# A fused attention, mixer and gated-MLP kernel: the first stage's order written out, later transposes, weight splits on VectorE

## The chip, the cores and the metric

The kernel runs on one core of a Trainium2 chip. The metric is the device time of one execution in microseconds. Engines are called by their names: TensorE (PE), VectorE (DVE), ScalarE (ACT), GpSimd (POOL), and SyncE (SP), which here issues all DMAs.

## The reference

Eight batches of 576 tokens go through three blocks. Block-local attention in chunks of 64 tokens gives x; a mixer multiplies over tokens and over channels; a gated MLP with a spatial product gives the output.

```python
scores = scale * np.matmul(q_c, k_c.transpose(0, 1, 2, 4, 3))   # 8 heads, 9 chunks of 64
attn = np.exp(scores - np.max(scores, axis=-1, keepdims=True))
attn = attn / (np.sum(attn, axis=-1, keepdims=True) + 1e-09)
x = np.matmul(attn, v_c)                                        # to [B, 576, 512]
h = np.maximum(x.transpose(0, 2, 1) @ w_tok1, 0.0) @ w_tok2     # tokens 576 -> 256 -> 576
u = x + h.transpose(0, 2, 1)
x = u + np.maximum(u @ w_ch1, 0.0) @ w_ch2                      # channels 512 -> 1536 -> 512
h = np.maximum(x @ w_in, 0.0)                                   # 512 -> 1024, halves u and v
v_s = np.einsum('ts,bsd->btd', w_spatial, normalized(v)) + b_spatial[None, :, None]
out = (u * v_s) @ w_out
```

## The kernel before

**Pairs of halves.** A product of 32-bit accuracy is made of three f16 products: every operand is kept as a high half and a low half (value minus high half), and high·high, high·low and low·high are summed in PSUM. The weights come in double precision: each is read as two 32-bit words, put together to an f32 by bit operations and then split. `add_w` cuts them into chunks `W[0]` to `W[23]`: 0 and 1 are `t1w` (first token product), 2 and 3 `t2w`, 4 to 9 `c1w` (first channel product), 10 to 15 `c2w`, 16 to 19 `inw` (gate), 20 and 21 `otw` (output), 22 and 23 `spw` (spatial). A chunk has four steps, one per `w_tick` with two chunks in flight: `upper` (two VectorE operations, L127 and L129), `lower` (one, L133), `high` (ScalarE, L139) and `low`. In chunks 0 to 5 `low` is made by TensorE, as f32 identity times s (L149) minus f16 identity times the high half (L150), and evicted by ScalarE (L151); from chunk 6 on by one VectorE operation (L144). Chunks 0 to 19 are loaded into tiles that are still unused (vn, otw, spw, xb, xT) and are split during batch 0's channel products; 20 to 23 are loaded into parts of hb and are split later.

**Attention.** A batch has five groups g of 128 tokens (the last of 64). The groups of batches 0 and 1 go through `wide_steps`: score (TensorE, L380), shift (VectorE, a maximum and a subtraction, L387 and L388), expo (ScalarE), norm (VectorE, L397 to L400), turn (TensorE transposes, L405), turned (ScalarE), attend (TensorE, L416 and L418), out_hi (ScalarE, L425 and L426) and out_lo (VectorE, L431). Later batches go through `at_steps`, with L246 as the score and L302 as the attend product. Batch 0's five groups come first in the program, each three ticks behind the one ahead. All further groups are a list `order` of (5g + s, g, s) that `a_step` works off one step at a time.

**Batches.** Per batch: tok1 (L500, L504), tok2 (L477 with t2w), ch1 (12 outputs of 24 products, L477 with c1w), ch2 (L560), gate_v (L477 with inw), then tok1 of the next batch, then `gated` (spatial and gate_u, L477), tok2 of the next batch and proj (L657). ch1's output is evicted by ScalarE (high half, L550) and VectorE (low half, L551). PSUM is a pool `pm` of four two-bank tiles, handed out in turn to all of this.

**What sets the order.** Inside `tc.manual_schedule` the named engines issue in the order in which the code is written: TensorE from tok1 on, and SyncE for the first loads. Into TensorE's written order `pump` inserts attention steps and weight ticks: each product moves a planner's clock on by its columns / 2.4 + 2.5 ns, and an entry of `pumps` runs its step when the clock has come to its due time. The other engines, and TensorE ahead of tok1, are ordered by a scheduler from the program's order as priority and its own estimate of when inputs are ready. Each engine then issues strictly in the order so fixed.

Of the kernel before, what the change touches and what calls it, by code (L numbers as in the profile page):

```python
# [26 lines left out]
def mixer_kernel(ctx: ExitStack, tc, qk0, qk, v, wt1, wt2, wc1, wc2, win, wsp, bsp, wout, out):  # L27
# [58 lines left out]
    neg = gall[:, 4864:4992]  # L86
    W = []

# [7 lines left out]
    early = lambda i: FIRST[i] if i < 6 else CYCLE[i % 3] if i < 20 else ("h0", "h1")[i % 2]  # L96
# [18 lines left out]
    def w_steps(i):  # L115
# [39 lines left out]
    KW, LATE, BY_PE = 2, 20, 6  # L155
# [192 lines left out]
    one_v = v32.rearrange("p a b c d -> p (a b c d)")[:, 0:512].rearrange("p (c h d) -> p c h d", c=2, h=4)  # L348
# [13 lines left out]
    def wide_steps(g):  # L362
# [3 lines left out]
        if b == 0:  # L366
            raw, vals = first_qk[:, i * 1024:i * 1024 + 8 * n], first_v[:, 2 * i:2 * i + nc_]
        else:
            raw, vals = one_qk[:, 0:8 * n], one_v[:, 0:nc_]
# [73 lines left out]
    order = sorted((KA * g + s, g, s) for g in range(NT, NG) for s in range(NA))  # L443
    todo = [0]

    def a_step():
# [4 lines left out]
        for f in live[g][s]:  # L451
            f()
# [40 lines left out]
    def tok1():  # L493
# [8 lines left out]
        for m in range(2):  # L502
            for e in range(2):
                PE.matmul(out=pss[m], lhsT=t1w[:, e, col(4, m)], rhs=x16[:, 8], start=False, stop=(e == 1))  # L504
                pump(DM)
            last = ACT.activation(out=h1[:, m, 0], in_=pss[m], func=AF.Relu).ins  # L506
            DVE.scalar_tensor_tensor(out=h1[:, m, 1], in0=pss[m], scalar=0.0, in1=h1[:, m, 0],  # L507
                                     op0=ALU.max, op1=ALU.subtract)
# [16 lines left out]
    def tok2(m, x):  # L525
# [8 lines left out]
        first_residual(ps, m, x)  # L534
# [9 lines left out]
    def ch1(m):  # L544
# [5 lines left out]
        ACT.activation(out=hh, in_=ps, func=AF.Relu)  # L550
# [130 lines left out]
    with tc.manual_schedule(engines={mybir.EngineType.SP}):  # L681
# [3 lines left out]
        for i in range(2, 5):  # L685
            wide_qk(i)
# [3 lines left out]
    for tick in range(3 * 4 + 9):  # L690
# [4 lines left out]
        if tick >= 9:  # L695
            w_tick()
# [120 lines left out]
```

## Time and profile before

| | |
|---|---|
| median of 3 runs | 1179.11 us (1178.23 to 1180.81) |
| the profiled execution | 1178.89 us |
| its span, first to last instruction | 1177.1 us |
| TensorE busy | 1132.4 us (96%) |
| VectorE busy | 719.0 us (61%) |
| ScalarE busy | 424.9 us (36%) |
| GpSimd busy | 197.7 us (17%) |

Rows of the timeline give the start, the duration, the engine, the line of the code, the operation, the tiles (out<-in), shapes and count; in brackets stands how long the engine was idle before it and whose end released it. In the names, `gb` is the scratch tile of the weight splits and holds the identity, `hb` the hidden activations (and at first batch 0's q, k and v), `mp` any PSUM tile, `sd` scores and probabilities, `p` and `pT` the transposed probabilities, `xb` the residual stream's halves. Windows give each engine's busy time (and instructions) in a stretch, then TensorE's granted clock as a share of full speed, the share of the DMA engines and GB/s.

### The profile page before, as it was taken

Reading aid. Unit: us, or ns where it says so; the run is one execution under the profiler, and the core shown is the slowest. Engines: PE = TensorE matmul, PEld = TensorE weight load, DVE = VectorE, ACT = ScalarE, POOL = GpSimd, SP = SyncE. Lnnn points to the kernel's source line nnn. Section 1 sums busy time; section 2 is a strip of 40 time slices with the busy share of each in tenths; the row PEclk is TensorE's granted clock in tenths of the full one; section 3 lists DMA queues with packets and bytes.
Section 4 is the critical chain, followed back from the end, with each engine's and each line's share of the span. In section 5 each row is a group of like instructions: output and inputs, shape, how many; then the busy total and the mean of one; then the engine's idle time right before and its main releaser. Section 6 shows DMA issues by size and latency. Waiting matters only on the chain. (4 is left out here: it accounts for less than half of the span.)

```text
span 1177.1 us, 22164 instructions
## 1 busy us (share of the span) xinstructions
PE 1132.4 (96%) x9564; PEld 819.1 (70%) x9564; DVE 719.0 (61%) x1279; ACT 424.9 (36%) x658; POOL 197.7 (17%) x186
## 2 busy tenths in 40 slices
PE   5879998999999999999999999999999999999998
PEld 4457755788577875778667885778757786677765
DVE  6899889755676655875576555765656432442141
ACT  3544434443335424443344333354233422221121
POOL 0000013201220122211131013201222011200020
PEclk9999999999999999999999999999999999999999
DMA  9456252312223230232223122233201311000001
GB/s 326 167 190 223 60 185 46 72 46 55 63 46 90 68 68 27 63 91 50 68 46 81 46 61 57 46 81 64 73 28 46 55 28 36 1 1 1 10 28 45
DMA packets 87602, 83.55 MB, mean 71 GB/s; under 512 B 66128, under 2 KB 68432, under 8 KB 85200
## 3 DMA queue, kind: packets, MB, share of 16 engines
q1 hardware_dynamic: 87504, 82.14, 26.1%
q8 instruction: 75, 1.23, 0.4%
q14 instruction: 23, 0.19, 0.1%
HBM read 58.52 MB, written 9.44 MB: 58 GB/s over the span
## 5 line engine op out<-in xcount | busy, mean ns | idle before, releaser
L477 PE MATMUL mp<-xb,c1w 128*128 128x288 f16 x2304 | 288.9, 287 | 0.0
L560 PE MATMUL mp<-hb,c2w 128*128 128x288 f16 x2304 | 287.7, 286 | 0.0
L477 PEld LDWEIGHTS <-c1w 128*128 128x128 f16 x2304 | 224.8, 98 | 58.1
L560 PEld LDWEIGHTS <-c2w 128*128 128x128 f16 x2304 | 223.5, 98 | 55.8
L551 DVE SCALAR_TENSOR_TENSOR hb<-mp,hb 128x576 f16<-128x576 f32 x96 | 72.3, 753 | 103.5 <-ACT hb L550 103.3
L477 PE MATMUL mp<-spw,vn 128*128 128x288 f16 x896 | 117.9, 288 | 2.7 <-DVE xT L317 2.7
L477 PEld LDWEIGHTS <-vn 128*128 128x128 f16 x896 | 87.1, 99 | 26.3 <-PE mp L477 4.1
L550 ACT ACTIVATE hb<-mp 128x576 f16<-128x576 f32 x96 | 62.2, 648 | 108.8 <-PE mp L477 108.5
L477 PE MATMUL mp<-xb,inw 128*128 128x288 f16 x768 | 99.3, 286 | 0.0
L657 PE MATMUL mp<-otw,gb 128*128 128x512 f16 x432 | 96.0, 379 | 0.0
L477 PEld LDWEIGHTS <-inw 128*128 128x128 f16 x768 | 75.2, 98 | 20.4
L477 PE MATMUL mp<-inw,xb 128*128 128x512 f16 x384 | 86.0, 383 | 2.6 <-ACT xb L522 2.5
L281 POOL TENSOR_TENSOR p<-sd,p 128x512 f16<-128x512 f32 (+1 forms) x30 | 34.6, 1155 | 282.3 <-ACT p L278 271.1
L333 POOL TENSOR_TENSOR xh<-xT,xh 128x512 f16<-128x512 f32 x24 | 32.1, 1336 | 289.7 <-ACT xh L330 255.4
L657 PEld LDWEIGHTS <-gb 128*128 128x128 f16 x432 | 42.1, 98 | 47.9
L477 PEld LDWEIGHTS <-xb 128*128 128x128 f16 x384 | 37.6, 98 | 49.5 <-ACT xb L522 2.9
L521 DVE SCALAR_TENSOR_TENSOR rt<-mp,xT 128x576 f32<-128x576 f32 x32 | 24.2, 757 | 74.6 <-PE mp L560 74.1
L292 DVE SCALAR_TENSOR_TENSOR v<-v,v 128x512 f16<-128x512 f32 (+1 forms) x60 | 36.5, 634 | 40.7 <-ACT v L288 40.3
L596 DVE BATCH_NORM_STATS2 st<-vt 128x6 f32<-128x512 f32 (+1 forms) x40 | 27.6, 690 | 45.9 <-ACT vt L590 45.6
L523 POOL TENSOR_TENSOR xb<-rt,xb 128x576 f16<-128x576 f32 x21 | 29.4, 1400 | 153.2 <-ACT xb L522 153.2
L643 ACT ACTIVATE gb<-gt 128x576 f16<-128x576 f32 x32 | 21.8, 682 | 88.0 <-DVE gt L641 87.7
L477 PE MATMUL mp<-t2w,hb 128*128 128x288 f16 x384 | 51.2, 286 | 1.1 <-ACT hb L506 0.4
(147 smaller groups left out, 1367.5 us busy)
## 6 DMA issues: line engine op xcount, KB each, us to landing
qk<-in_qk SPq DMA_DIRECT2D x28, 512.0 KB, 3.9
v<-in_v SPq DMA_DIRECT2D x48, 256.0 KB, 3.9
out<-o SPq DMA_DIRECT2D x31, 256.0 KB, 2.0
vn<-in_wc SPq DMA_DIRECT2D x4, 1024.0 KB, 5.2
otw<-in_wc SPq DMA_DIRECT2D x3, 1024.0 KB, 6.5
spw<-in_wc SPq DMA_DIRECT2D x3, 1024.0 KB, 4.9
v<-in_v SPq DMA_DIRECT2D x20, 128.0 KB, 2.7
hb<-in_qk SPq DMA_DIRECT2D x4, 512.0 KB, 8.0
```

Source lines behind the costliest of these rows:

```text
L281: POOL.tensor_tensor(out=p16[rows, :, 1], in0=m["sd"][rows], in1=p16[rows, :, 0], op=ALU.subtract)
L292: DVE.scalar_tensor_tensor(out=hi_lo[:, :, 1 + e], in0=v_in[:, :, e], scalar=SX, in1=hi_lo[:, :, 3 * e], op0=ALU.mult, op1=ALU.subtract)
L333: POOL.tensor_tensor(out=m["lo"], in0=xT[:, :, tk], in1=m["hi"], op=ALU.subtract)
L477: PE.matmul(out=o, lhsT=l, rhs=r, start=(i == 0), stop=(i == len(seq) - 1))
L521: DVE.scalar_tensor_tensor(out=t, in0=ps, scalar=DN10, in1=two(x[:, m]), op0=ALU.mult, op1=ALU.add)
L523: eng.tensor_tensor(out=xl, in0=t, in1=xh, op=ALU.subtract)
L550: ACT.activation(out=hh, in_=ps, func=AF.Relu)
L551: DVE.scalar_tensor_tensor(out=hlo, in0=ps, scalar=0.0, in1=hh, op0=ALU.max, op1=ALU.subtract)
L560: PE.matmul(out=o, lhsT=c2w[:, a, k, mc], rhs=hb[:, k, r, s], start=(k + e == 0), stop=(k == 11 and e == 2))
L596: DVE.bn_stats(out=st[0:n], in_=t[0:n])
L643: ACT.activation(out=gh, in_=t, func=AF.Copy)
L657: PE.matmul(out=ps, lhsT=gb[:, l, k, tk], rhs=otw[:, r, k], start=(k == 0 and e == 0), stop=(k == 3 and e == 2))
```

## The change

Ahead of the first token product the order of all of TensorE, ScalarE, VectorE and SyncE is now written out by hand, as `FIRST_ORDER`: two letters name a step (sc score, sh shift, ex expo, nm norm, tn turn, tu turned, at attend, oh out_hi, ol out_lo), the digit its group, `w` one weight tick. The loads of v are cut in two and stand between those of q and k. All low parts of weights are made on VectorE (now L142), and the f16 identity goes. Chunks 20 and 21 join the first set (`LATE` is 22) and are loaded into spw and vn. In batch 1 the transposes come three steps later, the attend products five, its v has two buffers, and from batch 2 on all attention steps are due 15 later, so that none is done during batch 1's: the stretches now have 100, 127, 100, ... steps instead of 127, 100, 100, .... Batch 1's attention, the two evictions of tok1 and of ch1, and the residuals of tok2 and ch2 get `tc.high_priority()`, above the weight splits. tok1 is written after the ticks of chunk 1, with a tick of weights per 1000 ns of the planner's clock during tok1 and tok2, and tok2 after those of chunk 3.

```diff
+    FIRST_ORDER = """sc0 sc1 sh0 ex0 sh1 ex1 sc2 nm0 tn0 tu0 sc3 sh2 ex2 at0 nm1 tn1 tu1 oh0 sh3 ex3 sc4 at1 nm2 tn2 tu2 ol0
+        oh1 sh4 ex4 at2 nm3 tn3 tu3 ol1 oh2 at3 w nm4 tn4 tu4 w ol2 oh3 at4 w ol3 w w oh4 w ol4"""
...
-    early = lambda i: FIRST[i] if i < 6 else CYCLE[i % 3] if i < 20 else ("h0", "h1")[i % 2]
+    early = lambda i: FIRST[i] if i < 6 else CYCLE[i % 3] if i < 22 else ("h0", "h1")[i % 2]
...
         def low():
-            if i >= BY_PE:
-                DVE.scalar_tensor_tensor(out=lo, in0=s, scalar=scale, in1=hi, op0=ALU.mult, op1=ALU.subtract)
-                return
-            ps, w = pm.tile([128, 2, 512], F32, tag="m", name="mp"), n // 2
-            for a in range(2):
-                c = slice(a * w, a * w + w)
-                PE.matmul(out=ps[:, a, 0:w], lhsT=eye, rhs=s[:, c], start=True, stop=False)
-                PE.matmul(out=ps[:, a, 0:w], lhsT=neg, rhs=hi[:, c], start=False, stop=True)
-            ACT.activation(out=lo.rearrange("p (a c) -> p a c", a=2), in_=ps[:, :, 0:w], func=AF.Copy, scale=scale)
+            DVE.scalar_tensor_tensor(out=lo, in0=s, scalar=scale, in1=hi, op0=ALU.mult, op1=ALU.subtract)
...
-    KW, LATE, BY_PE = 2, 20, 6
+    KW, LATE = 2, 22
...
-        steps = [[lambda: wide_qk(g)], [], [], []] + steps
-        steps[5].append(lambda: wide_v(b, 2 * i, vals))
-        return steps + [[]] * (NA - len(steps))
+        sc, sh, ex, nm, tn, tu, at, oh, ol = steps
+        return [[lambda: wide_qk(g)], [], [], [], sc, sh, ex, nm,
+                [lambda: wide_v(b, 2 * i, vals)], [], [], tn, tu, [], [], at, oh, ol, [], []]
...
-    order = sorted((KA * g + s, g, s) for g in range(NT, NG) for s in range(NA))
+    order = sorted((KA * g + s + 15 * (g >= 2 * NT), g, s) for g in range(NT, NG) for s in range(NA))
...
-        for f in live[g][s]:
-            f()
+        with tc.high_priority() if g < 2 * NT and s not in (0, 8) else nullcontext():
+            for f in live[g][s]:
+                f()
...
-        ACT.activation(out=hh, in_=ps, func=AF.Relu)
-        DVE.scalar_tensor_tensor(out=hlo, in0=ps, scalar=0.0, in1=hh, op0=ALU.max, op1=ALU.subtract)
+        with tc.high_priority():
+            ACT.activation(out=hh, in_=ps, func=AF.Relu)
+            DVE.scalar_tensor_tensor(out=hlo, in0=ps, scalar=0.0, in1=hh, op0=ALU.max, op1=ALU.subtract)
...
-    with tc.manual_schedule(engines={mybir.EngineType.SP}):
+    ET = mybir.EngineType
+    with tc.manual_schedule(engines={ET.SP, ET.PE, ET.Activation, ET.DVE}):
         wide_qk(0)
         wide_qk(1)
-        wide_v(0, 0, first_v)
-        for i in range(2, 5):
-            wide_qk(i)
+        wide_v(0, 0, first_v[:, 0:4])
+        wide_qk(2)
+        wide_v(0, 4, first_v[:, 4:9])
+        wide_qk(3)
+        wide_qk(4)
...
+        w_until(1)
+        pumps.append([clock[0], 1000.0, w_tick, lambda: wdone[0] < LATE])
         tok1()
+        w_until(3)
         attention_from(1, 0.0, 80000.0)
...
-                w_until(19)
-                pumps.pop()
+                w_until(21)
+                pumps.pop(0)
```

TensorE at the start of the first token product (tok1: L500 before, L492 now). Before, its products stand between those of the weights' low parts for c1w:

```order
181 L149 MATMUL mp<-gb 128x512
182 L150 LDWEIGHTS gb
183 L150 MATMUL mp<-c1w,gb 128x512
184 L149 MATMUL mp<-gb 128x512
185 L500 LDWEIGHTS t1w
186 L500 MATMUL mp<-x_94,t1w 128x512
187 L500 LDWEIGHTS t1w
188 L500 MATMUL mp<-x_94,t1w 128x512
189 L150 LDWEIGHTS gb
190 L150 MATMUL mp<-c1w,gb 128x512
191 L149 MATMUL mp<-gb 128x512
192 L150 LDWEIGHTS gb
```

Now:

```order
149 L407 MATMUL mp<-p_90,hb 64x64
150 L409 MATMUL mp<-hb,p_90 64x64
151 L407 MATMUL mp<-p_90,hb 64x64
152 L409 MATMUL mp<-hb,p_90 64x64
153 L492 LDWEIGHTS t1w
154 L492 MATMUL mp<-x_94,t1w 128x512
```

The token product follows at once on the last attend products (L407, L409) of batch 0, with no weight work between.

VectorE where the work on weights begins (the chunk in otw is chunk 1). Before, after the second group's low output (the first L431 below is the second in the program), chunk 1 runs among the third and fourth groups:

```order
26 L431 SCALAR_TENSOR_TENSOR x_94<-mp,x_94 128x512
27 L129 SCALAR_TENSOR_TENSOR gb<-otw,gb 128x640
28 L397 TENSOR_REDUCE mx<-sd 128x8
29 L133 SCALAR_TENSOR_TENSOR gb<-otw,gb 128x640
30 L398 TENSOR_SCALAR mx<-mx 128x8
31 L399 RECIPROCAL mx<-mx 128x8
32 L400 TENSOR_TENSOR sd<-sd,mx 128x512
33 L387 TENSOR_REDUCE mx<-mp 64x8
```

Now the second low output (L422) is followed by the first operation of chunk 0 (in vn), with all but the last norm done:

```order
28 L422 SCALAR_TENSOR_TENSOR x_94<-mp,x_94 128x512
29 L127 TENSOR_SCALAR gb<-vn 128x640
30 L129 SCALAR_TENSOR_TENSOR gb<-vn,gb 128x640
31 L388 TENSOR_REDUCE mx<-sd 64x8
32 L389 TENSOR_SCALAR mx<-mx 64x8
33 L390 RECIPROCAL mx<-mx 64x8
34 L391 TENSOR_TENSOR sd<-sd,mx 64x512
35 L133 SCALAR_TENSOR_TENSOR gb<-vn,gb 128x640
```

The weights moved behind the first four groups' norms.

VectorE near the end of batch 0's ch1. Its last two low halves (L551) before, among the chunks of inw (17 in spw):

```order
143 L129 SCALAR_TENSOR_TENSOR gb<-spw,gb 128x1024
144 L400 TENSOR_TENSOR sd<-sd,mx 128x512
145 L551 SCALAR_TENSOR_TENSOR hb<-mp,hb 128x576
146 L144 SCALAR_TENSOR_TENSOR inw<-gb,inw 128x1024
147 L133 SCALAR_TENSOR_TENSOR gb<-spw,gb 128x1024
148 L551 SCALAR_TENSOR_TENSOR hb<-mp,hb 128x576
```

Now (L546; the chunk in otw is 13):

```order
125 L546 SCALAR_TENSOR_TENSOR hb<-mp,hb 128x576
126 L378 TENSOR_REDUCE mx<-mp 128x8
127 L127 TENSOR_SCALAR gb<-otw 128x1024
128 L379 TENSOR_TENSOR sd<-mp,mx 128x2x4x64
129 L129 SCALAR_TENSOR_TENSOR gb<-otw,gb 128x1024
130 L388 TENSOR_REDUCE mx<-sd 128x8
131 L142 SCALAR_TENSOR_TENSOR c2w<-gb,c2w 128x1024
132 L422 SCALAR_TENSOR_TENSOR x_94<-mp,x_94 128x512
133 L389 TENSOR_SCALAR mx<-mx 128x8
134 L546 SCALAR_TENSOR_TENSOR hb<-mp,hb 128x576
```

The last low half of ch1 now stands four chunks earlier in the sequence of weights, between the chunks of c2w, and has eight other rows between it and the one before.

## Rows read from the trace of the kernel before

**Rows 1.** Page, busy time (share of the span) and instructions of each engine.

```profile
PE 1132.4 (96%) x9564; PEld 819.1 (70%) x9564; DVE 719.0 (61%) x1279; ACT 424.9 (36%) x658; POOL 197.7 (17%) x186
```

**Rows 2.** Windows of the first 300 us: PE, PEld, DVE, ACT, POOL; clock, DMA, GB/s.

```profile
0.00:18.00 18.00, 7.80 (x169) 6.70 (x169) 7.00 (x14) 4.82 (x7) 1.12 (x9) 1.00 0.94 272
18.00:54.00 36.00, 29.06 (x348) 18.29 (x348) 32.28 (x49) 19.19 (x30) 0.00 (x0) 0.86 0.65 241
...
60.00:135.00 75.00, 63.90 (x792) 50.19 (x790) 74.81 (x102) 31.14 (x45) 0.00 (x0) 0.98 0.52 177
...
160.00:196.50 36.50, 28.98 (x168) 14.90 (x166) 32.86 (x64) 15.91 (x24) 11.30 (x10) 0.91 0.22 69
196.50:300.00 103.50, 103.36 (x910) 81.33 (x911) 68.25 (x116) 40.77 (x63) 19.61 (x15) 1.00 0.31 67
```

**Rows 3.** Waits of TensorE, whole span: us in total, times, longest.

```profile
PE mp L405 <- DVE sd L400: 19.1, 7, 5.2
PE mp L302 <- DVE hb L507: 5.5, 5, 4.6
```

**Rows 4.** Windows of L149 alone, then L150 alone: PE, PEld; clock, DMA, GB/s.

```profile
0.00:60.00 60.00, 11.63 (x24) 4.58 (x24) 0.91 0.73 244
...
0.00:60.00 60.00, 4.25 (x12) 1.33 (x12) 0.91 0.73 244
```

**Rows 5.** Timeline of TensorE, up to 191 us.

```profile
4.79 1.13 PE L380 MATMUL mp<-hb 64*64 64x64 f32 x32 [4.79 <-DMA hb<-in_qk]
...
52.99 1.03 PE L504 MATMUL mp<-x,t1w 128*128 128x512 f16 x4
...
67.88 0.98 PE L405 MATMUL mp<-gb,sd 128*128 128x128 f32 x4 [5.16 <-DVE sd L400]
...
83.36 0.63 PE L405 MATMUL mp<-gb,sd 128*128 128x128 f32 x4 [1.82 <-DVE sd L400]
...
101.98 0.69 PE L380 MATMUL mp<-qk 64*64 64x64 f32 x32
...
104.06 0.32 PE L416 MATMUL mp<-pT,v 64*64 64x64 f32 x2
...
105.77 8.38 PE L477 MATMUL mp<-xb,c1w 128*128 128x288 f16 x67
...
159.76 1.46 PE L477 MATMUL mp<-inw,xb 128*128 128x512 f16 x6
163.68 1.04 PE L477 MATMUL mp<-inw,xb 128*128 128x512 f16 x2 [2.45 <-ACT xb L522]
...
190.64 0.83 PE L302 MATMUL mp<-pT,v 128*128 128x64 f16 x16 [4.59 <-DVE hb L507]
```

**Rows 6.** Groups of VectorE, 60 to 135 us: busy us, mean ns | idle before.

```profile
L551 DVE SCALAR_TENSOR_TENSOR hb<-mp,hb 128x576 f16<-128x576 f32 x12 | 9.0, 753 | 0.0
L144 DVE SCALAR_TENSOR_TENSOR c2w<-gb,c2w 128x1024 f16<-128x1024 f32 x6 | 7.3, 1221 | 0.0
...
L388 DVE TENSOR_TENSOR sd<-mp,mx 128x512 f32<-128x512 f32 (+1 forms) x5 | 3.4, 687 | 0.0
...
L127 DVE TENSOR_SCALAR gb<-otw 128x1024 uint32<-128x1024 uint32 x4 | 2.8, 688 | 0.0
...
L399 DVE RECIPROCAL mx<-mx 128x8 f32<-128x8 f32 (+1 forms) x5 | 1.0, 197 | 0.0
```

**Rows 7.** Timeline of VectorE: three places of the start, and batch 1's ch1.

```profile
5.99 0.69 DVE L387 TENSOR_REDUCE mx<-mp 128x8 f32<-128x512 f32 x1 [5.99 <-PE mp L380]
...
16.86 0.69 DVE L431 SCALAR_TENSOR_TENSOR x<-mp,x 128x512 f16<-128x512 f32 x1 [4.14 <-ACT xT L426]
17.46 0.68 DVE L387 TENSOR_REDUCE mx<-mp 128x8 f32<-128x512 f32 x1
18.06 0.48 DVE L127 TENSOR_SCALAR gb<-vn 128x640 uint32<-128x640 uint32 x1
...
237.60 0.76 DVE L551 SCALAR_TENSOR_TENSOR hb<-mp,hb 128x576 f16<-128x576 f32 x1 [2.18 <-ACT hb L550]
```

More of the change, by code (lines that the diff above doesn't have):

```diff
@@ L1 @@
-from contextlib import ExitStack
+from contextlib import ExitStack, nullcontext
 import concourse.bass as bass
@@ L505, in tok1 @@
                 pump(DM)
-            last = ACT.activation(out=h1[:, m, 0], in_=pss[m], func=AF.Relu).ins
-            DVE.scalar_tensor_tensor(out=h1[:, m, 1], in0=pss[m], scalar=0.0, in1=h1[:, m, 0],
-                                     op0=ALU.max, op1=ALU.subtract)
+            with tc.high_priority():
+                last = ACT.activation(out=h1[:, m, 0], in_=pss[m], func=AF.Relu).ins
+                DVE.scalar_tensor_tensor(out=h1[:, m, 1], in0=pss[m], scalar=0.0, in1=h1[:, m, 0],
+                                         op0=ALU.max, op1=ALU.subtract)
         return last
@@ L533, in tok2 @@
         products(outs, seq)
-        first_residual(ps, m, x)
+        with tc.high_priority():
+            first_residual(ps, m, x)
     def three(w_hi, w_lo, n, mov):
@@ L564, in ch2 @@
         for i, m in enumerate(ms):
-            residual(pss[i][1], m, x, DVE if m == 3 or len(ms) > 1 else POOL)
-            DVE.tensor_copy(out=xt[:, m], in_=xb[:, :, m, 512:576])
+            with tc.high_priority():
+                residual(pss[i][1], m, x, DVE if m == 3 or len(ms) > 1 else POOL)
+                DVE.tensor_copy(out=xt[:, m], in_=xb[:, :, m, 512:576])
     def gate_u(m):
@@ L677, in mixer_kernel @@
     POOL.memset(mhalf, -0.5)
-    for t, fill in ((eye, 1.0), (neg, -1.0 / SW)):
-        POOL.memset(t, 0.0)
-        POOL.affine_select(out=t, in_=t, compare_op=ALU.not_equal, fill=fill, base=0, pattern=[[-1, 128]], channel_multiplier=1)
-    with tc.manual_schedule(engines={mybir.EngineType.SP}):
+    POOL.memset(eye, 0.0)
+    POOL.affine_select(out=eye, in_=eye, compare_op=ALU.not_equal, fill=1.0, base=0, pattern=[[-1, 128]], channel_multiplier=1)
+    ET = mybir.EngineType
+    with tc.manual_schedule(engines={ET.SP, ET.PE, ET.Activation, ET.DVE}):
         wide_qk(0)
         wide_qk(1)
-        wide_v(0, 0, first_v)
-        for i in range(2, 5):
-            wide_qk(i)
+        wide_v(0, 0, first_v[:, 0:4])
[3 more added lines that the diff above has]
+        wide_qk(4)
         for _ in range(6):
             w_next()
-    steps = [wide_steps(i) for i in range(5)]
-    for tick in range(3 * 4 + 9):
-        for i in range(5):
-            if 0 <= tick - 3 * i < 9:
-                for f in steps[i][tick - 3 * i]:
-                    f()
-        if tick >= 9:
-            w_tick()
-    w_until(5)
+        steps = [wide_steps(g) for g in range(5)]
+        names = ("sc", "sh", "ex", "nm", "tn", "tu", "at", "oh", "ol")
+        for word in FIRST_ORDER.split():
+            if word == "w":
+                w_tick()
+            else:
+                for f in steps[int(word[2])][names.index(word[:2])]:
+                    f()
     SP.dma_start(out=bB, in_=bsp)
@@ L714, in mixer_kernel @@
             if b == 0:
-                pumps.append([clock[0], 1700.0, w_tick, lambda: wdone[0] < LATE])
+                pumps[0][1] = 1700.0
             for m in range(12):
```

6 lines of the change are left out of this document (3 added, 3 removed).

## The prediction, made before the changed kernel ran

> **What bounds the kernel now.** First the page's shares: TensorE is busy for 1132.4 of 1177.1 us [rows 1], so 44.7 us of idle time and the work itself are all there is to win. Then the windows by stage: where does that idle lie? TensorE is busy 7.80 of the first 18 us, 29.06 of the next 36, 63.90 of 75 between 60 and 135, 28.98 of 36.5 between 160 and 196.5, and 103.36 of 103.5 after it [rows 2]: nearly all idle time lies in the first 200 us. In the same rows VectorE is the full engine: 32.28 of 36 us, then 74.81 of 75. So the start is bound by VectorE, which turns the weights into pairs of halves, and by the order in which TensorE meets its results. The waits say it by name: 19.1 us for L405, the transposes of the first two attentions, behind VectorE's L400, and one of 4.6 us at L302 [rows 3].
>
> **Low parts on VectorE.** TensorE loses the products of L149 and L150, 11.63 and 4.25 us busy [rows 4], and ScalarE their evictions. They stood ahead of the first token product (first order listing), which ends at 54.02 [rows 5]. VectorE gains six low parts: two of 640, two of 576, two of 1024 columns. By the 512-wide 0.69 and the 1024-wide 1.22 [rows 6] they cost some 0.8, 0.74 and 1.22 each, 5.5 us on the full engine.
>
> **The start.** VectorE's first instruction stays at 5.99 [rows 7]. Ahead of the first weight chunk now stand five shifts (two 512-wide each), four norms (two wide, two narrow of 0.2) and two low outputs: 6.9 + 7.1 + 1.4 = 15.4 us [rows 6]. With no waits that ends at 21.4. Before, it was busy 7.00 of these first 12 us, up to 18 [rows 2]; at that share it ends at 32.4. I take 24.5, nearer the first end: the 4.14 us in which VectorE stood at L431 for the first group's output [rows 7] are what the new order fills with the next groups' shifts, while the third and fourth scores still wait for loads that stand behind half and all of v. Swapping these loads adds no bytes, so the weight chunks land as before.
>
> From there I count VectorE's rows up to the low part of the first chunk of c1w, which the first channel product needs. Four small chunks (0.47 + 3 x 0.77) are 11.1; chunk 4 (0.69 + 3 x 1.22) 4.35; half of chunk 5 1.91; a norm, three low outputs, a shift and most of a norm 6.3; two hidden lows 1.4; eight residual steps of 0.75 6.0: 31.1 us in 44 instructions. Independent ones start 0.60 apart though they last 0.69 [rows 7], so I take 0.07 off each: 28.0. So 24.5 + 28.0 = 52.5. The token product has its two chunks at about 34.5 on the same count and ends near 38, against 54.02. Before, TensorE stood from 62.7 to 67.88 at the fifth group's transposes, with 9 of the 288 first channel products done [rows 5]; now it stands at the weights until 52.5, with some 4 done.
>
> **Transposes later.** In batch 1 the transposes move three steps back and the attention products five; L405 after 9 channel products becomes L396 after 70, the next goes from 81 to 181. Of the four waits of [rows 5] and its kind (5.16, 1.82 and two near 2) none should be left: 70 products in, near 60 us, the norm has been done since 53. What is late next is the eviction: the pool has four PSUM tiles, and the first pair of second channel products needs the tile that channel product 11 leaves. Its low part (L546) now stands behind chunk 13's first half (third listing). From 52.5 to it: the second half of chunk 5, chunks 6 to 12 and half of 13 are 34.8 us, twelve low parts at 0.75 9.0, three groups of attention 10.7: 54.5, less 63 x 0.07 = 50.1, that is 102.6. TensorE gets there earlier: 284 products at 0.125 (8.38 over 67 [rows 5]) 35.5, three scores at 0.69, two transposes at 0.63 and two attends at 1.71 (from 104.06 to 105.77) 6.7, so 94.7, with small waits 96. It waits some 6 us, where before it had 11 us of waits.
>
> From 102.6 the first pair takes 138 x 0.125 + 2.8 of attention = 20.1, to 122.7. Its last chunk, 15, is on VectorE at 52.5 + 63.0 = 115.5 (68.4 us in 77 instructions), in time by 4 us. The second pair takes 18.0 + 3.7, to 144.4, against 159.76 plus no wait before [rows 5].
>
> **Chunks 20 and 21 early.** Output weights now precede gate and spatial work on VectorE: with 16 to 21, one low part of spatial weights, group 9, residuals and a little of batch 2, 38.7 us in 45 instructions, less 3.2: the last half of xb stands at 115.5 + 35.5 = 151. So the gate's third block goes on at about 150.5; before it went on at 164.89, after a wait of 2.45 [rows 5]. That is a lead of 14.4 us. Of it 0.9 is no gain: two score products of batch 2, 0.46 each, come later.
>
> **After the gate.** The 4.59 us at 190.64 are a PSUM tile that VectorE's L507 frees [rows 3, 5]; L507 now has priority, and VectorE has one chunk less in that stretch, so the wait goes, and 0.3 behind it. Batch 2's attention has 127 steps in its stretch instead of 100. There TensorE is full and VectorE has 68.25 of 103.5 busy [rows 2]: a quarter more of its attention fits. I put 1 us against it, from 0 to 6.
>
> **Sum.** 14.4 - 0.9 + 4.9 - 1 = 17.4. Check by another way: TensorE loses some 15 us of work (11.63 + 4.25, less overlap), and of its 36.5 us of idle time up to 200 some 33 stay: 13 before the token product, 8 around the second, 6 at the pair, 6 at the gate. That gives 18.5. The profiled execution took 1178.89 us, 1.8 more than its span and 0.2 less than the median of three: 1178.9 - 17.4 = 1161.5, say 1161.
>
> [...] The clock row says 1.00 for the first 18 us, though TensorE is busy for less than half [rows 2]. [...] As a case of this kernel, from rows alone: three attends at 1.71 x 1.13 / 0.69 = 2.8 instead of 1.71 put VectorE's start 3.3 us later and the time at 1164.3; I give this 0.2 of the 0.62 below.
>
> **Rivals.** (a) Forecast, 1155 to 1167, with the case just named: 0.62. (b) The moved waits come back: TensorE's order is counted in products, not in time, and VectorE has 5.5 us more to do. If the four transposes of batch 1 wait as before, 11 us beside the new 6, the time is 1172. For it: VectorE is full throughout. Against: the norms lead the transposes by 7 us or more in my count. 0.10. (c) Batch 2's denser attention makes TensorE wait, five groups at about 1.2: 1167 to 1168; against it the 35 us that VectorE has free there [rows 2]. 0.12. (d) Slower: lock-step. VectorE takes its rows strictly in turn: L387 started at 17.46 [rows 7], only after the waiting L431. The twelve low parts and four residuals now stand at the place that priority gave them, ahead of weights. If TensorE is late at each, VectorE stands there, the weights are late, and TensorE is late again. In a later batch VectorE stands 2.18 us for one such low part [rows 7]; sixteen of these are 35 us on an engine without slack, 1196; from 1.1 us each it is slower than before. Against: by my count TensorE is ahead at all twelve. 0.07. [...] (e) Better: the tile wait at the pair doesn't arise, or the start is near 21.4: 1152 to 1155. 0.09. The change does what it says in the order listings, so that rival has no weight of its own.
>
> **Numbers.** 0.2%, 2.4 us, is about what can be told from no change. Slower holds (d), 0.07; within 0.2% lies only a mix of (b), (c) and part of (d), 0.03; faster 0.90. The range leaves out (d) and the outer half of (b) and (e): 1154 to 1171.
>
> **What would show it.** Right: the first token product ends near 38, no L149-like products; L396 has no wait in batch 1; the first long wait in channel work ends near 52 at c1w's low part, the next near 102 at L546; the gate goes on near 150; no wait at the first batch-2 products. Wrong: the first weight chunk on VectorE later than 28, VectorE idle between 25 and 150, or TensorE idle by more than 3 us in all between 200 and 350.

## The result and the profile after

The changed kernel takes 1167.28 us (median of 4 runs, 1166.05 to 1167.75) against 1179.96 us measured beside it (1178.23 to 1181.54): a ratio of 0.9891, 95% interval 0.9874 to 0.9909. That is 12.7 us faster by the medians, inside the range of 1154 to 1171, and 6.3 us short of the 1161 forecast. The profiled execution took 1167.75 us with a span of 1165.9, against 1178.89 and 1177.1: 11.2 us of span.

The page's busy shares and the windows of the first 300 us (columns as in [rows 1] and [rows 2]):

```profile
PE 1125.4 (97%) x9528; PEld 814.1 (70%) x9528; DVE 725.1 (62%) x1285; ACT 419.6 (36%) x652; POOL 195.1 (17%) x184
```

```profile
0.00:18.00 18.00, 8.07 (x197) 7.09 (x197) 8.16 (x15) 3.77 (x5) 0.73 (x7) 1.00 0.94 287
18.00:54.00 36.00, 26.16 (x369) 17.56 (x368) 32.72 (x53) 16.37 (x29) 0.00 (x0) 0.95 0.62 224
54.00:60.00 6.00, 3.85 (x17) 2.43 (x18) 5.97 (x10) 1.06 (x1) 0.00 (x0) 0.56 0.00 0
60.00:135.00 75.00, 70.99 (x793) 55.30 (x792) 74.49 (x97) 30.35 (x42) 0.00 (x0) 0.97 0.61 207
...
160.00:196.50 36.50, 36.50 (x282) 25.11 (x281) 31.27 (x63) 13.06 (x21) 11.86 (x11) 1.00 0.15 38
196.50:300.00 103.50, 99.65 (x853) 73.98 (x852) 74.86 (x132) 46.68 (x73) 20.42 (x15) 0.98 0.35 84
```

Between 60 and 135 us TensorE is now busy for 70.99 instead of 63.90, between 160 and 196.5 for all instead of 28.98 of 36.50. Between 196.5 and 300, where it had been full, it is busy for 99.65 of 103.50: something is lost there. The removed products took up to 15.9 us [rows 4], but TensorE's busy time fell by 7.0 only, 1132.4 to 1125.4. Busy time is not a sum of work: it counts products that overlap once (the rows from 215.65 to 222.88 us in the kernel before, below, last 7.89 us together and are 7.13 us of busy time), and products at a lower clock for as long as they take (experiment 4, at 0.75 instead of 0.86 between 18 and 54 us, has the case).

TensorE's waits (us in total, times, longest), which answer to [rows 3]:

```profile
PE mp L371 <- DMA hb<-in_qk: 9.9, 4, 4.7
PE mp L469 <- DVE c1w L142: 4.6, 1, 4.6
PE mp L396 <- DVE x L422: 2.7, 2, 1.7
```

The transposes' 19.1 us behind the norm and the 5.5 us of L302 have gone from the head of this list. In their place stand the first scores' loads, 9.9 us where the kernel before waited 5.3, and the wait for the first weights of the first channel product. The transposes still wait, but for PSUM tiles that L422 frees. The same places in TensorE's timeline, from the first token product to the gate's third block:

```profile
39.01 1.03 PE L496 MATMUL mp<-x,t1w 128*128 128x512 f16 x4
...
50.91 0.65 PE L469 MATMUL mp<-xb,c1w 128*128 128x288 f16 x4
56.16 7.67 PE L469 MATMUL mp<-xb,c1w 128*128 128x288 f16 x40 [4.59 <-DVE c1w L142]
...
100.25 0.90 PE L555 MATMUL mp<-hb,c2w 128*128 128x288 f16 x6
101.34 2.38 PE L555 MATMUL mp<-hb,c2w 128*128 128x288 f16 x18 [0.19 <-DVE sd L379]
104.80 0.66 PE L396 MATMUL mp<-gb,sd 128*128 128x128 f32 x4 [1.08 <-DVE x L422]
...
123.77 0.66 PE L555 MATMUL mp<-hb,c2w 128*128 128x288 f16 x4 [1.08 <-DVE sd L379]
126.09 0.92 PE L396 MATMUL mp<-gb,sd 128*128 128x128 f32 x4 [1.66 <-DVE x L422]
...
150.72 0.61 PE L469 MATMUL mp<-inw,xb 128*128 128x512 f16 x2 [0.54 <-ACT xb L515]
153.46 10.49 PE L469 MATMUL mp<-inw,xb 128*128 128x512 f16 x40 [2.14 <-DVE xb L516]
```

The token product ends at 40.04, 14.0 us earlier than in [rows 5]; the second channel product starts at 100.25 instead of 117.52, and the gate's third block goes on at 153.46 instead of 164.89, a lead of 11.4.

Further on, the second token product of batch 1: first the kernel before, then the changed one.

```profile
215.65 1.88 PE L477 MATMUL mp<-t2w,hb 128*128 128x288 f16 x14
217.36 0.63 PE L302 MATMUL mp<-pT,v 128*128 128x64 f16 x16
217.83 2.49 PE L477 MATMUL mp<-t2w,hb 128*128 128x288 f16 x19
220.16 0.63 PE L246 MATMUL mp<-kt,qt 128*128 128x64 f16 x16
220.62 2.26 PE L477 MATMUL mp<-t2w,hb 128*128 128x288 f16 x15
222.72 1.46 PE L657 MATMUL mp<-otw,gb 128*128 128x512 f16 x6
```

```profile
198.14 2.61 PE L469 MATMUL mp<-t2w,hb 128*128 128x288 f16 x20
201.54 0.63 PE L293 MATMUL mp<-pT,v 128*128 128x64 f16 x16 [0.79 <-DVE gt L627]
...
203.25 1.51 PE L469 MATMUL mp<-t2w,hb 128*128 128x288 f16 x11 [0.59 <-DVE gt L637]
205.81 0.63 PE L237 MATMUL mp<-kt,qt 128*128 128x64 f16 x16 [1.05 <-DVE xT L507]
...
207.98 2.80 PE L469 MATMUL mp<-t2w,hb 128*128 128x288 f16 x12 [1.43 <-DVE xT L507]
210.58 5.89 PE L653 MATMUL mp<-otw,gb 128*128 128x512 f16 x24
```

The lead is 215.65 - 198.14 = 17.5 where this product starts and 222.72 - 210.58 = 12.1 where it ends. Four new waits, 3.86 us in all, are most of that loss. Behind the last of them the 12 products take 2.80 us where experiment 2, with the same waits, needs 1.63, and the 24 of the projection (L653) take 5.89 against 5.34 in the kernel before (L657). The granted clock is 0.50 from 209 to 210.6 us.

### The profile page after: what moved, and what is told of

The parts are those of the page before. It is cut to its first block, busy times and chain, and to the rows that moved or that the text cites. A ratio compares the mean times of both kernels' runs of the same rounds, so it can differ in the third digit from the quotient of the medians.

```text
span 1165.9 us, 22091 instructions
## 1 busy us (share of the span) xinstructions
PE 1125.4 (97%) x9528; PEld 814.1 (70%) x9528; DVE 725.1 (62%) x1285; ACT 419.6 (36%) x652; POOL 195.1 (17%) x184
## 5 line engine op out<-in xcount | busy, mean ns | idle before, releaser
L546 DVE SCALAR_TENSOR_TENSOR hb<-mp,hb 128x576 f16<-128x576 f32 x96 | 72.4, 754 | 96.7 <-ACT hb L545 96.5
L545 ACT ACTIVATE hb<-mp 128x576 f16<-128x576 f32 x96 | 61.8, 645 | 105.9 <-PE mp L469 105.7
L653 PE MATMUL mp<-otw,gb 128*128 128x512 f16 x432 | 96.6, 381 | 0.0
L653 PEld LDWEIGHTS <-gb 128*128 128x128 f16 x432 | 42.3, 98 | 48.7 <-issue 0.8
L469 PE MATMUL mp<-t2w,hb 128*128 128x288 f16 x384 | 53.6, 296 | 4.3 <-DVE t2w L142 1.7
L600 POOL TENSOR_TENSOR y<-z,mhalf 128x1 f32<-128x1 f32 (+1 forms) x40 | 22.3, 557 | 209.8 <-DVE z L599 209.8
L592 DVE BATCH_NORM_STATS2 st<-vt 128x6 f32<-128x512 f32 (+1 forms) x40 | 27.6, 691 | 44.4 <-ACT vt L586 44.1
```

The source lines that it names most:

```text
L469: PE.matmul(out=o, lhsT=l, rhs=r, start=(i == 0), stop=(i == len(seq) - 1))
L546: DVE.scalar_tensor_tensor(out=hlo, in0=ps, scalar=0.0, in1=hh, op0=ALU.max, op1=ALU.subtract)
L592: DVE.bn_stats(out=st[0:n], in_=t[0:n])
L600: POOL.tensor_tensor(out=y[0:n], in0=z[0:n], in1=mhalf[0:n], op=ALU.pow)
L653: PE.matmul(out=ps, lhsT=gb[:, l, k, tk], rhs=otw[:, r, k], start=(k == 0 and e == 0), stop=(k == 3 and e == 2))
```

## The experiments

Each ratio is to the kernel before measured beside the kernel in question; differences between experiments are taken between these ratios (0.1% is 1.2 us).

**1. Batch 1's transposes early again.** From the changed kernel; the load of v moves with them.

```diff
-        return [[lambda: wide_qk(g)], [], [], [], sc, sh, ex, nm,
-                [lambda: wide_v(b, 2 * i, vals)], [], [], tn, tu, [], [], at, oh, ol, [], []]
+        return [[lambda: wide_qk(g)], [], [], [lambda: wide_v(b, 2 * i, vals)], sc, sh, ex, nm,
+                tn, tu, at, oh, ol, [], [], [], [], [], [], []]
```

> From the changed kernel (1167.3 us), batch 1's transposes and attend products go back to their old steps; its v loads come two steps earlier. Theory (later transposes are worth what the old waits cost): waits at L396 in batch 1 come back, near 5, 2, 2 and 2 us, 1174 to 1178 us. Rival (the old waits were only the late start; VectorE's norms now lead anyway and the waits that are left come from PSUM tiles): L396 waits under 3 us in all, 1166 to 1169 us.

Measured: 1168.77 us, ratio 0.9899 (0.9884 to 0.9915). At batch 1's transposes no wait came back. So where they stand is worth nothing that can be measured once the norm ahead of them has priority.

**2. No priority anywhere.** From the changed kernel, at all five places:

```diff
-        with tc.high_priority():
+        with nullcontext():
```

> From the changed kernel (1167.3 us), every high priority is taken away, so that the scheduler ranks evictions, residuals and batch 1's attention as the program's order does. Theory (priority is what frees the token product's PSUM tile in time, and keeps the evictions ahead of weights): the wait of some 4 to 5 us at the first score or attend product of batch 2 comes back, 1171 to 1174 us. Rival (that wait went because VectorE has less weight work beside the gate): no such wait, 1166 to 1169 us.

Measured: 1183.73 us, ratio 1.0022 (1.0010 to 1.0034). Without priority the rest of the change is slower than the kernel before; priority is worth 1.3%, 15.5 us. TensorE's waits begin right behind the first token product:

```profile
46.99 1.62 PE L469 MATMUL mp<-t2w,hb 128*128 128x288 f16 x6 [3.53 <-DVE hb L500]
51.59 4.26 PE L469 MATMUL mp<-t2w,hb 128*128 128x288 f16 x17 [2.98 <-DVE hb L500]
65.98 0.64 PE L469 MATMUL mp<-xb,c1w 128*128 128x288 f16 x2 [5.36 <-ACT xb L508]
```

The 4.59 us that the kernel before waited at batch 2's first products did not come back, though: the change does not need priority to remove them.

**3. Batch 2's attention not later.** From the changed kernel. Batch 2's v then lands in v's buffer ahead of the last attend products of batch 1, which multiply other values; the products stay the same in number and shape.

```diff
-    order = sorted((KA * g + s + 15 * (g >= 2 * NT), g, s) for g in range(NT, NG) for s in range(NA))
+    order = sorted((KA * g + s, g, s) for g in range(NT, NG) for s in range(NA))
```

> From the changed kernel (1167.3 us), the delay of 15 for all attention steps from batch 2 on is taken away, so that 27 of them run in batch 0's stretch again. Theory (the 27 moved steps are what makes TensorE wait 3.9 us in the second batch's tok2): those waits shrink below 1.5 us, but the steps come back where VectorE is full, so 1164 to 1168 us. Rival (VectorE's full stretch pays for them): 1170 to 1174 us, with the gate's third block later by 3 us or more.

Measured: 1180.08 us, ratio 0.9994 (0.9985 to 1.0003): without these 15 steps the whole gain is gone. TensorE stands once for long, behind VectorE's last row (L230) for the first score of batch 2, and one wait at batch 2's attend products is back in part:

```profile
143.43 1.03 PE L237 MATMUL mp<-kt,qt 128*128 128x64 f16 x16 [18.28 <-DVE qt L230]
...
191.62 0.63 PE L293 MATMUL mp<-pT,v 128*128 128x64 f16 x16 [2.30 <-DVE hb L500]
```

These rows of VectorE have no priority and stand between chunks of inw: L228 starts at 134.92, L229 at 138.37, L230 at 142.95. Whether priority for them would do what the 15 steps do was not tried. The four waits in the second token product of batch 1 are absent here, so they are the price of the later, denser steps.

**4. Low parts on VectorE alone.** From the kernel before.

```diff
-    KW, LATE, BY_PE = 2, 20, 6
+    KW, LATE, BY_PE = 2, 20, 0
```

> From the kernel before (1179.1 us), only the low parts of chunks 0 to 5 are moved to VectorE; no order written out, no later transposes, no priority. Theory (the hand-written start order makes the gain, low parts alone cost VectorE 5.5 us and spare TensorE products that stood beside its waits): 1176 to 1184 us. Rival (taking these products out of TensorE's way is itself most of the gain): 1168 to 1172 us.

Measured: 1188.21 us, ratio 1.0073 (1.0054 to 1.0092), slower. Its busy times and waits:

```profile
PE 1133.0 (95%) x9528; PEld 819.8 (69%) x9528; DVE 723.8 (61%) x1285; ACT 421.0 (35%) x652; POOL 198.0 (17%) x186
```

```profile
PE mp L405 <- DVE sd L400: 25.8, 9, 4.3
...
PE mp L477 <- ACT xb L522: 4.7, 1, 4.7
```

Its first token product ends at 47.48, 6.5 us earlier than before, and its gate starts at 169.42, 9.7 us later (159.76 in [rows 5]). TensorE lost work that it had time for; VectorE, which was full up to 135 us, got six low parts more, and four of batch 1's five transposes wait longer (2.82, 4.31, 3.46 and 2.94 us, before 1.82, none, 2.17 and 1.96), the first one less (2.83, before 5.16). TensorE has 36 products less and is busy 0.6 us longer, 1133.0 against 1132.4: what is left runs at a lower clock, 0.75 between 18 and 54 us and 0.91 between 60 and 135, where the kernel before has 0.86 and 0.98 [rows 2]. How much of the 0.73% is this clock and how much VectorE's waits, no run separates.

**5 and 6. The start: three `sd` buffers; the first attend product ahead of the fourth score.** Both from the changed kernel. VectorE's first waits there, with the first weight chunk:

```profile
15.56 0.69 DVE L378 TENSOR_REDUCE mx<-mp 128x8 f32<-128x512 f32 x1 [0.81 <-PE mp L371]
19.11 0.69 DVE L379 TENSOR_TENSOR sd<-mp,mx 128x512 f32<-128x512 f32 x1 [2.87 <-PE mp L396]
...
26.03 0.48 DVE L127 TENSOR_SCALAR gb<-vn 128x640 uint32<-128x640 uint32 x1
```

```diff
-    sdp = ctx.enter_context(tc.tile_pool(name="sdp", bufs=2))
+    sdp = ctx.enter_context(tc.tile_pool(name="sdp", bufs=3))
```

> The changed kernel with three buffers instead of two for `sd` (scores and probabilities). The changed kernel's first weight chunk starts on VectorE at 26.03 us, not at 24.5, and in its start VectorE stands 2.87 us at the subtract L379 until the transposes L396 of the group two ahead have read the same `sd` buffer. Theory: these two buffers are what my count of the start left out; with three the 2.87 goes, the first chunk starts near 23.5 to 24.5, the token product ends near 38 instead of 40.0, the first channel product goes on near 54 instead of 56.2, and the time is 1165 to 1166 (ratio to the kernel before near 0.9875). Rival: the wait only moves to the next thing that is late, the products of score, transposes and attend in their written order and the loads behind them (TensorE stands 2.66 and 2.12 us for loads at 10.1 and 14.4); then the first chunk starts within 0.5 us of 26.0 and the time is 1167 to 1168.

```diff
-    FIRST_ORDER = """sc0 sc1 sh0 ex0 sh1 ex1 sc2 nm0 tn0 tu0 sc3 sh2 ex2 at0 nm1 ...
+    FIRST_ORDER = """sc0 sc1 sh0 ex0 sh1 ex1 sc2 nm0 tn0 tu0 sh2 ex2 at0 sc3 nm1 ...
```

> The changed kernel with one step moved in the written order of the start: the first group's attend product and the second shift and exponent stand ahead of the fourth group's score, which waits 2.12 us for its load at 14.37 us. Theory: in a written order the attend product pays for a load that it doesn't need; ahead of the score it ends some 2 us earlier, VectorE reaches the first weight chunk near 24 instead of 26.03, and the time is 1165 to 1166. Rival: VectorE then waits for the fourth score instead, which starts later by the attend product's 2 us or so; the first chunk starts between 25.5 and 28 and the time is 1167 to 1169.

Measured: 1165.57 us (ratio 0.9881, 0.9868 to 0.9893) with the first chunk at 24.76 us; 1164.77 us (0.9872, 0.9859 to 0.9885) with it at 25.58. With three buffers the 2.87 us are gone and TensorE goes on with the first channel product at 53.82 instead of 56.16: the two buffers were the wait that my count of the start left out. In time that is 0.1% and 0.2%; the intervals overlap the changed kernel's, so no gain is shown.

**7. Batch 2's steps paused over that token product.** From the changed kernel.

```diff
-                attention_from(b + 2, 0.0, 118000.0)
+                attention_from(b + 2, 24000.0 if b == 0 else 0.0, 94000.0 if b == 0 else 118000.0)
```

> The changed kernel with batch 2's attention steps started only 24 us of the planner's clock after the place where they start now, so that none stands inside the second token product of batch 1, and put closer together behind it (94 us instead of 118 for the 127 steps). Theory: the waits of 0.79, 0.59, 1.05 and 1.43 us between 201 and 208 us in the changed kernel, which the kernel before doesn't have, come from batch 2's steps on VectorE and ScalarE standing among the token product's evictions and residuals; without them there these waits go and the time falls by 2 to 4 us, to 1163 to 1165. Rival: the denser steps behind it make TensorE wait about as much again there, and the time is 1166 to 1169.

Measured: 1171.09 us, ratio 0.9921 (0.9908 to 0.9935). The four waits are gone, and two others stand in their place: this one, and 3.44 us a batch later, at 319.95, where attend products (L293) stand for VectorE's L500 (0.40 at that place in the changed kernel).

```profile
211.94 0.74 PE L237 MATMUL mp<-kt,qt 128*128 128x64 f16 x16 [3.48 <-DVE qt L229]
```

Between 196.5 and 300 us TensorE is busy for 100.02 instead of 99.65. The rival held, and more: the denser steps wait about as much as the four waits they replace. Ahead of the later L500 VectorE works through the gate's normalization and stands for GpSimd's L600 there (1.48, 1.43, 0.66, 1.43 and 0.66 us); why that is later than in the changed kernel is not shown.

**8. Chunks 20 and 21 late again.** From the changed kernel, with the same limit in `early` and ahead of the gate.

```diff
-    KW, LATE = 2, 22
+    KW, LATE = 2, 20
...
-                w_until(21)
+                w_until(19)
```

> The changed kernel with chunks 20 and 21 (output weights) taken out of the early set again (`LATE` 20): they are loaded into hb and split after the gate's start, as before. Two steps of my prediction hang on them: that they delay the residuals ahead of the gate's third block, and that VectorE then has one chunk less in the stretch where the wait of 4.59 us for L507 stood. Theory: the wait at the first products of batch 2 is gone because batch 2's steps are due later (with them early it came back as 3.2 us), not because of the chunks; then the gate's third block goes on 1 to 3 us earlier, at 151 to 152.5 instead of 153.5, the wait stays away, and the time is 1165 to 1167. Rival: VectorE with two chunks more behind the gate is late for the spatial product's or batch 2's work again; TensorE waits 3 to 5 us between 165 and 200, and the time is 1169 to 1172.

Measured: 1167.51 us, ratio 0.9888 (0.9869 to 0.9906), no difference. The wait stays away, as the theory had it, so not the chunks removed it. But the gate's third block goes on 98.3 us after the first channel product (58.29 to 156.58), against 97.3 (56.16 to 153.46): the two chunks delayed nothing there.

**9. Priority alone.** From the kernel before; the attention's loads excepted, as in the change.

```diff
-        for f in live[g][s]:
-            f()
+        for i, f in enumerate(live[g][s]):
+            with tc.high_priority() if g < 2 * NT and s and (s, i) != (5, 1) else nullcontext():
+                f()
...
-        ACT.activation(out=hh, in_=ps, func=AF.Relu)
-        DVE.scalar_tensor_tensor(out=hlo, in0=ps, scalar=0.0, in1=hh, op0=ALU.max, op1=ALU.subtract)
+        with tc.high_priority():
+            ACT.activation(out=hh, in_=ps, func=AF.Relu)
+            DVE.scalar_tensor_tensor(out=hlo, in0=ps, scalar=0.0, in1=hh, op0=ALU.max, op1=ALU.subtract)
...
```

and so for tok1's evictions and the residuals.

> The kernel before with one part of the change: `tc.high_priority()` on batch 1's attention, on the evictions of the first token and the first channel product and on the residuals behind the second ones. The low parts on TensorE, the old start, the early transposes and the set of 20 early chunks stay. Without priority the changed kernel took 1183.7 us. Theory: priority on VectorE alone is what wins, since VectorE is the full engine up to 150 us: the waits of TensorE for the first hidden halves and residuals around the second token product go, and the 19.1 us at the transposes L405 fall, since the norm ahead of them has priority too; the time is 1166 to 1173 (ratio near 0.990). Rival: priority only pays with the later transposes and the written start, because in the old order the transposes stand 9 products behind the norm's start and TensorE stands at them whatever VectorE prefers; and work taken ahead of weights makes the weights later; the time is 1176 to 1184 (ratio 0.997 to 1.003).

Measured: 1173.90 us, ratio 0.9947 (0.9934 to 0.9960): nearly half of the gain. Its waits, against [rows 3]:

```profile
PE mp L405 <- DVE sd L400: 10.7, 6, 3.7
PE mp L302 <- DVE hb L509: 5.4, 5, 4.5
```

The transposes, where they were, wait 10.7 us instead of 19.1, and all of the difference is batch 1's: its waits are 1.15, 1.13 and 0.50 instead of 5.16, 1.82, 2.17 and 1.96, 2.8 us instead of 11.1. The wait at L302 is untouched.

**10. No priority on ch1's evictions.** From the changed kernel.

```diff
-        with tc.high_priority():
-            ACT.activation(out=hh, in_=ps, func=AF.Relu)
-            DVE.scalar_tensor_tensor(out=hlo, in0=ps, scalar=0.0, in1=hh, op0=ALU.max, op1=ALU.subtract)
+        ACT.activation(out=hh, in_=ps, func=AF.Relu)
+        DVE.scalar_tensor_tensor(out=hlo, in0=ps, scalar=0.0, in1=hh, op0=ALU.max, op1=ALU.subtract)
```

> The changed kernel with `tc.high_priority()` taken from the evictions of the first channel product alone (ScalarE's high and VectorE's low half of its twelve outputs); the first token product's evictions, the residuals and batch 1's attention keep it. Without any priority the changed kernel lost 16.4 us. Theory: most of that was lost around the second token product, where the weights went ahead of hidden halves and residuals (3.5, 3.0, 5.4 and 1.7 us); the twelve evictions are worth little, 1 to 5 us: 1168 to 1172. Rival: the four PSUM tiles are the bound, each eviction that stands behind a chunk of weights (about 4.4 us) holds TensorE up; then 8 to 16 us are lost, 1175 to 1183.

Measured: 1178.41 us, ratio 0.9983 (0.9974 to 0.9993). Of the 1.3% of priority, 0.9%, 10.9 us, lies in these twelve evictions. VectorE's first three low halves and, behind them, TensorE:

```profile
63.06 0.75 DVE L545 SCALAR_TENSOR_TENSOR hb<-mp,hb 128x576 f16<-128x576 f32 x1
...
74.53 0.74 DVE L545 SCALAR_TENSOR_TENSOR hb<-mp,hb 128x576 f16<-128x576 f32 x1
...
79.20 0.75 DVE L545 SCALAR_TENSOR_TENSOR hb<-mp,hb 128x576 f16<-128x576 f32 x1
```

```profile
80.00 0.69 PE L371 MATMUL mp<-qk 64*64 64x64 f32 x32 [1.82 <-DVE hb L545]
...
84.60 1.14 PE L469 MATMUL mp<-xb,c1w 128*128 128x288 f16 x4 [3.56 <-DVE sd L379]
92.36 0.47 PE L407 MATMUL mp<-pT,v 64*64 64x64 f32 x2 [6.62 <-DVE hb L545]
```

The low halves come 11.5 and 4.7 us apart, with chunks of weights between. A low half holds one of the four PSUM tiles, and all of TensorE's work draws on these: scores and attend products stand 1.82 and 6.62 us behind low halves, and a channel product 3.56 behind a score's subtraction (L379) that stands among the same chunks. Behind L545 alone TensorE stands 11.5 us up to the second channel product, which starts at 121.12 instead of 100.25; about half of that comes back later. My theory of 1 to 5 us fell; the rival's tiles are the mechanism.

**11. The start of the kernel before.** The changed kernel with the groups three ticks apart and only SyncE written out.

```diff
-    with tc.manual_schedule(engines={ET.SP, ET.PE, ET.Activation, ET.DVE}):
+    with tc.manual_schedule(engines={ET.SP}):
...
-        for word in FIRST_ORDER.split():
-            if word == "w":
-                w_tick()
-            else:
-                for f in steps[int(word[2])][names.index(word[:2])]:
-                    f()
+    for tick in range(3 * 4 + 9):
+        for i in range(5):
+            if 0 <= tick - 3 * i < 9:
+                for f in steps[i][tick - 3 * i]:
+                    f()
+        if tick >= 9:
+            w_tick()
```

> The changed kernel with the start of the kernel before: groups three ticks apart, a tick of weights per tick from the tenth on, and TensorE, ScalarE and VectorE ordered by the scheduler instead of by the written order; the loads, the low parts on VectorE and all else stay as changed. Theory: the written order is worth what VectorE no longer stands for in the first 20 us (the 4.14 us at the first low output, and smaller waits), 3 to 6 us, and the first token product ends near 44 instead of 40.0: 1170 to 1174. Rival: the start pays back nothing, because VectorE takes the same rows in another order and the weights for the first channel product end when they end, near 56; then the time is 1166 to 1169.

Measured: 1163.53 us (1160.81 to 1165.85), ratio 0.9856 (0.9834 to 0.9877): not slower than the changed kernel, and the fastest of all, though its interval still touches the other's. TensorE:

```profile
46.10 1.03 PE L496 MATMUL mp<-x,t1w 128*128 128x512 f16 x4
...
54.24 2.15 PE L469 MATMUL mp<-xb,c1w 128*128 128x288 f16 x14
57.42 3.84 PE L469 MATMUL mp<-xb,c1w 128*128 128x288 f16 x30 [1.03 <-DVE xb L509]
...
97.70 0.90 PE L555 MATMUL mp<-hb,c2w 128*128 128x288 f16 x6
```

Its window (columns as in [rows 2]):

```profile
54.00:60.00 6.00, 4.86 (x40) 3.59 (x37) 6.00 (x12) 3.06 (x5) 0.00 (x0) 1.00 0.13 49
```

The written order ends the token product at 40.04 instead of 47.13 and loses all 7 us by the first channel product. There the changed kernel has 4 products done and goes on at 56.16; this one has 14 done and goes on at 57.42, 1.26 us later, which is ten products' time: they are level. VectorE does the same rows in both; here it does the weights first (the first c1w low part starts at 44.12, not at 54.93) and the residuals last. And the wait is 1.03 us, not 4.59: the 30 products behind it take 3.84 us, while the 40 of the changed kernel take 7.67, 2.7 more than at 0.125 each. The second channel product starts at 97.70, 2.55 us ahead of the changed kernel. For the first loads TensorE stands 5.4 us here, not 9.9, and for batch 0's norms 9.1 us, which the written order spares it: it trades one wait for another. Both theory and rival expected a time of 1166 or more.

**12. Both edits of the start**, experiments 5 and 6 in one kernel.

```diff
-    sdp = ctx.enter_context(tc.tile_pool(name="sdp", bufs=2))
+    sdp = ctx.enter_context(tc.tile_pool(name="sdp", bufs=3))
...
-    FIRST_ORDER = """sc0 sc1 sh0 ex0 sh1 ex1 sc2 nm0 tn0 tu0 sc3 sh2 ex2 at0 nm1 ...
+    FIRST_ORDER = """sc0 sc1 sh0 ex0 sh1 ex1 sc2 nm0 tn0 tu0 sh2 ex2 at0 sc3 nm1 ...
```

> The changed kernel with both changes of the start: three `sd` buffers and the first attend product ahead of the fourth group's score. Each alone gave 1165.6 and 1164.8 us, with the first weight chunk at 24.8 and 25.6 us. Theory: they remove different waits (2.87 us for the buffer, 2.12 for the load), so together the chunk starts near 23.5 to 24.3 and the time is 1163 to 1164.5. Rival: both remove the same wait, since the attend product held back the transposes that free the buffer; the chunk starts near 24.8 and the time is 1164.5 to 1166.

Measured: 1164.82 us, ratio 0.9867 (0.9849 to 0.9885), no further gain. The first chunk starts at 25.71 us: with the buffer freed VectorE stands 2.36 and 2.21 us for the third and fourth scores, whose loads came later in this run.

## Why the prediction was right, and where not

The direction was right and the mechanism of the engine that bounds the start too, but the forecast's reasons for the gain were largely the wrong ones. That the time lies in the range is in part luck. Without priority (experiment 2) or without batch 2's delay (experiment 3) nothing is gained, and the prediction names the first as a danger and the second as a cost; its counts only follow the order that both had made. The written start, the later transposes and the removed products, which it names as the gain, give nothing that the runs show. Its terms:

| step | predicted | measured |
|---|---|---|
| first weight chunk on VectorE | 24.5 | 26.03 |
| from there to the first c1w low part | 28.0 | 30.07 |
| first token product ends | 38 | 40.04 |
| second channel product starts | 96 | 100.25 |
| waits for tiles at the pair | 6, at one place | 4.0, in four waits |
| lead at the gate's third block | 14.4 | 11.4 |
| from there to batch 1's second token product | -0.9 + 4.9 | 17.5 - 11.4 = +6.1 |
| batch 2's denser attention | -1 (0 to -6) | 11.2 - 17.5 = -6.3 to the end |
| sum, of the span | 17.4 | 11.2 |

**The start** came as forecast in kind: TensorE stands at the first c1w weights with 4 products done. It was mis-sized by 1.5 us at its first chunk: I had counted VectorE's rows and the loads, not the two `sd` buffers (experiment 5). The case of three attends at 2.8 us each was an estimate from the first score products (1.13 us against 0.69 [rows 5]), and no run shows it for all three: the first attend takes 2.78 us (from 15.25 us), the second 2.53, the third 1.79. Of the 2.07 us more in the count, 1.35 are two waits of VectorE for TensorE inside it, at an attend product (0.36) and at the second token product (0.99).

**What a wait costs behind itself** was left out. TensorE's clock is granted at 0.56 between 54 and 60 us, behind the 4.59 us of idleness, and at 0.50 from 56.2 to 60 us: the 40 products behind the wait take 7.67 us, 2.7 more than at 0.125 each, on top of the wait. From the resume to the second channel product I had 43.5 us and it took 44.1, so my count of that stretch was some 2 us too long and hid the loss. In experiment 11, with 1.03 us of idleness, the same window has a clock of 1.00, and so it has in experiment 3, where TensorE waits 2.0 us for the residual (L509). The length of one wait does not decide it alone: at 208 us the clock fell (0.63 in the next microsecond) after waits of 1.05 and 1.43 us, with TensorE busy for 1.53 of the 4 us from 204, and in experiment 2 it stayed at 1.00 (196.5 to 300 us) after nearly the same waits, 1.13 and 1.43 us.

**The tile wait** came in other places and shorter. No wait is put down to L546; the four are for L379 and L422. The gate's third block waits for xb (L516) as the count had it; the count had 151, the sum took 150.5.

**Later transposes** were given the credit for 11 us of waits. They wait no more for the norm, as said, but not because they moved: put back they do not wait either (experiment 1), and with priority alone batch 1's wait 2.8 instead of 11.1 us (experiment 9). The sign "L396 has no wait in batch 1" failed, by 2.7 us for tiles.

**Low parts on VectorE** were entered as removed work. Alone they cost 0.73% (experiment 4). The cross-check by removed work, 18.5, took some 15 us off TensorE's busy time; it fell by 7.0 in the changed kernel, and not at all where these products alone went (1133.0, experiment 4). Whether these low parts help or cost within the changed kernel was not tried.

**Priority** stood in the prediction as a danger, rival (d), and as a reason for one wait, that at L302. VectorE did not stand at these rows (busy for 74.49 of 75 us between 60 and 135), and priority carries 1.3% in the changed kernel, most of it in ch1's evictions.

**The 4.59 us at L302** went, as forecast, but for neither reason given: it stays away without priority (experiment 2) and without the chunks' early place (experiment 8), and with priority alone it stands (4.5 us, experiment 9). With batch 2's steps early it comes back to half (experiment 3). In the changed kernel the attend products that stood there come only at 201.54. So it is where these steps lie; what halved it in experiment 3 is not shown.

**Batch 2's denser attention**, -1, is the term that failed most. VectorE's free 35 us were an average over 103.5 us; the loss lies in 10 us of the second token product, where L507, L627 and L637 are late. By the prediction's own sign, "TensorE idle by more than 3 us in all between 200 and 350", the term was wrong: TensorE is busy for 145.15 of these 150 us. Rival (c), at 1167 to 1168, had the right size with the waits in another place: four in that product, not one per group. Of the last 0.9 us, between 12.1 at its end and 11.2 at the program's, 0.55 are the projection behind it at the lower clock (0.62 from 210.6 to 212 us); the rest stays open. The delay that causes this is also worth 1.0% (experiment 3), which the prediction did not see.

So the gain is a balance: on the chip, priority alone is worth 0.5%, low parts alone cost 0.7%, the steps of batch 2 are worth 1.0% within the whole; the written start, the transposes' place and the two early chunks give nothing that can be measured. These parts are not shown to add up: the delay without the rest and the ticks of weights around the token products were not tried alone.

## What to carry to other kernels

Where a second engine is full, first order its queue by who waits on each row: an eviction that frees one of few PSUM tiles goes ahead of work that is only needed later. For twelve evictions this was worth 0.9% here, and removing 36 products from TensorE, by itself, nothing. A lead early in the program counts only where the next meeting of the two engines comes earlier too; follow VectorE's rows up to it, and see how long TensorE stands there, for it can be slower afterwards: 4.59 us of standing cost 2.7 more, 1.03 none. Moving work from an engine with slack to the full one can cost more than its own duration: here 8.6 us (0.73%) for 4.8 us more of VectorE's busy time.

## What the runs showed of the hardware

The granted clock's row of the first 18 us says 1.00 in every kernel, while 32 score products take 1.13 us there (at 4.69 us in the changed kernel) against 0.69 later (at 95.83). Durations differ where the row does not: four transposes take 1.11 us at 17.96 in the changed kernel and 0.66 at 22.37, both at a row of 1.00, and 0.65 at 18.19 with three `sd` buffers.

```profile
17.96 1.11 PE L396 MATMUL mp<-gb,sd 128*128 128x128 f32 x4
```

```profile
18.19 0.65 PE L396 MATMUL mp<-gb,sd 128*128 128x128 f32 x4
```

What sets these durations is not shown. The waits of the first scores for their loads differ from kernel to kernel at the same order of loads: 9.9 us in all in the changed kernel, 13.0 in experiment 8, where TensorE goes on with the first channel product at 58.29 us instead of 56.16.
